# Row numbers stored later, a shorter entry to the expert search, and the first tokens turned in halves

## The chip, the cores and the metric

The kernel runs on one core of a Trainium2 chip. The metric is the time of one execution on the device, in microseconds (us). The engines are TensorE (PE in the profile, with its weight loads as PEld), VectorE (DVE), ScalarE (ACT), GpSimd (POOL) and SyncE (SP), which here only issues transfers.

## The reference

Three layers follow one another; all arrays are float32 except the dense weights, which arrive as float64.

```
attention: B=2, H=8, S=768, D=64: each query sees keys within 16 places of it and 24 block maxima
x = attention output as [N=1536, 512]
logits = x @ w_gate                       # [1536, 8]
greedy over all (token, expert) pairs in order of -logits: a token takes the expert
    if neither is used up (192 tokens per expert)
for e: y[tokens of e] = relu(x[tokens of e] @ w1[e]) @ w2[e]      # 512 -> 1024 -> 512
h = y @ w_in ; g = 0 below -1, h above 1, (h+1)^2/4 between ; out = g @ w_out   # 512 -> 2048 -> 512
```

## The kernel before

**Attention** (`attention`) works on 12 tiles of 128 tokens. Its order on every engine is the hand-written list ORDER: each entry issues a few instructions, and an engine runs its own in that order. For the last tiles the list has `x_turn` (four transposes of a finished 128x512 tile on PE), `x_store` (the tile to memory, SP), `x_out` (the transposed tile out of PSUM), `logits` (32 small products on PE) and `logits_out` (8 columns of the tile `lg`). `later 0` and `later 1` in that list build the constants of the router.

**The router** (`Router`) replaces the greedy loop by eight phases, each of which closes one expert. `scale` finds the largest absolute logit: a reduction on DVE (L482), a transpose on PE (L484), a reduction of one row (L487), a product that spreads the result over the partitions (L489), then `best` (five DVE operations, L506 to L514, that find each token's best expert) and two operations that make the factor `r` (L494, L495). `phase` then finds the closing threshold in five digits of base 32. For each digit DVE makes masks (L677), PE counts them with 12 small products (L565), DVE makes flags (L569, L572), and one more product (L575) returns the digit. After the fifth digit the phase finds the expert's members, loads the expert's number into a register, and computes the 192 row numbers `idx` (L686 on PE, L688 on ACT).

**The gather** (`Experts.fetch`): POOL issues two indirect transfers (L717, 96 rows of 2 KB each) that bring the expert's tokens from `xdram`. Beside them SP stores the row numbers to `idxd` in memory (L719, 192 pieces of 4 bytes). For the first expert SP then issues a tiny transfer out of the gathered tile (L723), which makes SP wait until the second half has landed; the rest of the expert's weights are issued behind it (L745, L747). The first half quarter of them (L744) goes out as soon as the expert is known.

**The experts** (`run_experts`): the generator `products` makes the 64 products of each expert (each shows as two instructions, a few of them L776 and L785). PE gets its order from PLAN: at every step of the router (but those named half, best, left, places) one number of PLAN is read. Until `turns`, the count of steps since the first gather was issued, passes WAIT, that many blank products (`idle`, L709: 128x512, bfloat16, result never read) fill PE; after it, that many products of the experts are issued. So PE's queue holds search and experts interleaved, and it runs in that order. The first tokens are turned by `turn(0)` at the first step past WAIT: three blanks, four transposes (L757), three blanks, four transposes, each half taken out of PSUM by ACT (L758).

**The dense layers** (`FeedForward`) take 16 steps `s`, the first half of the tokens in steps 0 to 7. Their raw weights are loaded by SP (L922, L925) and turned into float32 on DVE. `run` loads the row numbers back as `idxo` (L1208); the results are scattered to their rows by indirect transfers on POOL (L1067), the first of them after step 7.

Pools of tiles reuse memory of pools that were closed: the router's and the experts' pools lie where attention's tiles lay. The first tile of such a pool waits for everything that touched the memory under the whole pool, attention's stores of `xs` to `xdram` among it.

Of the kernel before, what the change touches and what calls it, by code (L numbers as in the profile page):

```python
# [8 lines left out]
F32 = mybir.dt.float32  # L9
# [15 lines left out]
N = B * S  # L25
DM = H * D
NT = N // 128
E = 8
# [7 lines left out]
PLAN = """  # L36
2 5 2 1 2 2 2 2 2 2 2 2 2 1 10 10 3 3 3 3 3 2 4 2 2 2 2 9 9 2 3 3 3 3 3 3 3 3 2 2 16 9 3 3 3 3 3 3 3 3 3 2 2 10
12 2 3 3 3 3 3 3 3 3 2 2 10 9 3 4 3 3 4 3 3 3 3 2 2 10 9 2 3 3 3 4 3 3 3 3 2 2 10 9 12 3
"""

WAIT = 8

# [54 lines left out]
9 1 dve; pv 11 0; x_out 8 act; pv 9 1; sums 11 0 act; norm 11 0; logits 8; sums 9 1 act; pv_out 11 0; norm 9 1;  # L97
logits_out 8 act; x_store 11; x_turn 11; pv_out 9 1; x_out 11 dve; x_turn 9; x_store 9; x_out 9 act; logits 11;
logits 9; logits_out 11 dve; logits_out 9 dve
"""  # L100


def attention(tc, ctx, C, q, k, v, wg, xdram, lg, later, order=ORDER):
# [238 lines left out]

    def x_turn(t):
        p = live["xp", t] = ptr()
        for c in range(4):
            nc.tensor.transpose(p[:, c], live["x", t][:, c * 128:(c + 1) * 128], ident)  # L346
# [4 lines left out]

    def logits(t):
        p = live["l", t] = ptr()
        for c in range(4):
            for w in range(2):
                r = slice(64 * w, 64 * w + 64)
                nc.tensor.matmul(p[r, 0, :64], live["xt", t][:, c, r], wg[:, c], start=(c == 0), stop=(c == 3))
# [4 lines left out]
    def begin():  # L362
        warm = st.tile([128, 512], BF, name="warm")
        nc.vector.memset(warm, 0.0)
        for _ in range(9):
            nc.tensor.matmul(ptr().rearrange("p a b -> p (a b)"), warm[:, :128], warm, start=True, stop=True)

        rel = st.tile([128, 96], F32, name="rel")
        for h in range(2):
            nc.gpsimd.iota(rel[64 * h:64 * h + 64], pattern=[[1, 96]], base=-16, channel_multiplier=-1,  # L370
                           allow_small_or_imprecise_dtypes=True)
        for b in range(B):
            nc.gpsimd.memset(VW[b * G][:32, 0, :, :D], 0.0)
            nc.gpsimd.memset(VW[b * G + G - 1][64:96, 3, :, :D], 0.0)
            nc.gpsimd.memset(KW[b][:, 0, :, 0, :16], 0.0)
            nc.gpsimd.memset(KW[b][:, G - 1, :, 3, 80:96], 0.0)
        nc.vector.tensor_copy(identb, ident)
        nc.vector.memset(eps, 1e-9)

        nc.vector.memset(blocks, 0.0)  # L380
        nc.vector.tensor_reduce(blocks[:, 22:24], ident[:96, 16:80].rearrange("p (b k) -> p b k", k=32), axis=AX.X, op=OP.add)
        nc.vector.tensor_reduce(strips, ident.rearrange("p (k r) -> p r k", k=4)[:, :NB], axis=AX.X, op=OP.add)
        nc.vector.tensor_tensor(rel, rel, rel, op=OP.mult)
        for j in range(3):
            nc.vector.tensor_scalar(bias[j][:, :96], rel, 256.0, NEG, op0=OP.is_ge, op1=OP.mult)
            nc.vector.memset(bias[j][:, 96:], 0.0)

        nc.vector.memset(bias[0][:64, :16], NEG)
        nc.vector.memset(bias[2][64:, 80:96], NEG)
# [17 lines left out]
class Router:  # L407
# [15 lines left out]
    def open(self, ctx):  # L423
        self.wk = ctx.enter_context(self.tc.tile_pool(name="rt_work", bufs=2, side="right"))
        self.pp = ctx.enter_context(self.tc.tile_pool(name="rt_psum", bufs=2, space=PSUM, side="right"))

    def consts(self):
# [26 lines left out]
        self.ones = st.tile([1, 128], F32, name="ones")  # L454
        g.memset(self.ones, 1.0)
        self.left = st.tile([128, E], F32, name="left")
# [18 lines left out]
    def ps(self):  # L475
        return self.pp.tile([128, 512], F32, name="rt")

    def scale(self):

        nc, wk, lg = self.nc, self.wk, self.lg  # L480
        m = wk.tile([128, 1], F32, name="m")
        nc.vector.tensor_reduce(m, lg, axis=AX.XY, op=OP.max, apply_absolute_value=True)  # L482
        p = self.ps()
        nc.tensor.transpose(p[:1, :128], m, self.C["ident"])  # L484
        yield "scale"
        m2 = wk.tile([1, 1], F32, name="m2")
        nc.vector.tensor_reduce(m2, p[:1, :128], axis=AX.X, op=OP.max)  # L487
        p = self.ps()
        nc.tensor.matmul(p[:, :1], self.ones[:1], m2, start=True, stop=True)  # L489
        yield "scale"  # L490
        v = yield from self.best(lg)
        half = KARY / 2
        r = wk.tile([128, 2], F32, name="r")
        nc.vector.tensor_scalar(r[:, 0:1], p[:, :1], 1.0 / (half - 0.25), 1e-36, op0=OP.mult, op1=OP.max)  # L494
        nc.vector.reciprocal(r[:, 1:2], r[:, 0:1])  # L495

        self.v0 = wk.tile([128, NT], F32, name="v0")
        nc.vector.tensor_scalar(self.v0, v, r[:, 1:2], half, op0=OP.mult, op1=OP.add)
        self.r = r

# [17 lines left out]
    def phase(self, k):  # L518
# [13 lines left out]
        if not last:  # L532
            oh = self.oh
            for j in range(LEVELS):
# [25 lines left out]
                if k == 0 and j == 0:  # L560
                    nc.vector.tensor_scalar(Z, self.lg, self.r[:, 1:2], KARY / 2, op0=OP.mult, op1=OP.add)
                yield "mask" if j else "first"
# [128 lines left out]
class Experts:  # L691


    def __init__(self, tc, ctx, C, xdram, w1, w2, router, ff, idxd, spare, xp):
        self.tc, self.nc, self.C, self.spare = tc, tc.nc, C, spare
        self.x, self.w1, self.w2, self.rt = xdram, w1, w2, router
        self.ff, self.idxd, self.xp = ff, idxd, xp
        self.quarters = 0
        self.post = []
        self.wk = ctx.enter_context(tc.tile_pool(name="ex_work", bufs=2))  # L700
        self.pp = ctx.enter_context(tc.tile_pool(name="ex_psum", bufs=2, space=PSUM))
        self.W, self.XG, self.XT, self.number = {}, {}, {}, {}
# [8 lines left out]
    def fetch(self, k):  # L711
# [4 lines left out]
        for h in range(2):  # L716
            nc.gpsimd.indirect_dma_start(out=self.XG[k][:, h], out_offset=None, in_=self.x,  # L717
                                         in_offset=bass.IndirectOffsetOnAxis(ap=idx[:, h:h + 1], axis=0))
        nc.sync.dma_start(bass.AP(tensor=self.idxd.tensor, offset=self.idxd.offset + k // 4 * (N // 2) + k % 4 * 96,  # L719
                                  ap=[[1, 96], [HALF, 2]]), idx)  # L720
        if k == 0:
# [75 lines left out]
def run_experts(router, ex, ff, leave, plan=PLAN):  # L797
# [37 lines left out]

    def turn(k):
        for h in range(2):
            if k == 0:
                ex.idle(3)
            ex.transposed(k, h)  # L840
        turned[0] = k + 1

# [23 lines left out]
    for r in route():  # L866
# [7 lines left out]
        if turns > WAIT:  # L874
            for _ in range(n):
                next(run, None)
        else:
            ex.idle(n)
    for n, _ in enumerate(run):
        if n % TAIL == 0 and not ff.busy:  # L880
            next(conversions, None)
# [3 lines left out]
class FeedForward:  # L885
# [6 lines left out]

    def __init__(self, tc, ctx, C, w_in, w_out, idxd, out):
        self.tc, self.nc, self.ctx = tc, tc.nc, ctx
        self.w_in, self.w_out, self.idxd, self.out = w_in, w_out, idxd, out
        self.st = ctx.enter_context(tc.tile_pool(name="ff_static", bufs=1))
# [201 lines left out]
    def early(self, spare):  # L1098

        nc, tc = self.nc, self.tc  # L1100
        self.wk = self.ctx.enter_context(tc.tile_pool(name="ff_work", bufs=2, side="right"))
        self.pp = self.ctx.enter_context(tc.tile_pool(name="ff_psum", bufs=2, space=PSUM, side="right"))
        self.half = self.st.tile([128, 1], F32, name="half")
# [20 lines left out]
    def steps(self):  # L1124
# [6 lines left out]
        for s in range(2 * P):  # L1131
            outer = self.outer(s - 1, order) if s else iter(())
            ph, sided, summed = {}, 0, 0
            for n, j in enumerate((0, 1, 4, 6, 2, 3, 5) if s == 0 else range(7)):
                if s == 0 and j in (4, 6):
# [59 lines left out]
        for t in (3, 4, 5, 0, 1, 2):  # L1195
            h = t // 3
            for _ in self.outer(2 * P - 1, ((0, h, (t,)), (1, h, (t,)))):
                pass

    def run(self, ctx):  # L1200
        nc, tc = self.nc, self.tc
        self.ww = ctx.enter_context(tc.tile_pool(name="ff_split", bufs=3))
        self.op = ctx.enter_context(tc.tile_pool(name="ff_out", bufs=1, space=PSUM))
        for i in range(2):
            for _ in self.split(0, i):
                pass
        idx = self.idx = self.st.tile([128, NT], I32, name="idxo")
        nc.sync.dma_start(idx, bass.AP(tensor=self.idxd.tensor, offset=self.idxd.offset, ap=[[1, 128], [128, NT]]))  # L1208
        for _ in self.work:
# [3 lines left out]
def build(tc, q, k, v, w_gate, w1, w2, w_in, w_out, out):  # L1213
    nc = tc.nc
    with ExitStack() as ctx:
# [17 lines left out]
        with ExitStack() as c1:  # L1233
            attention(tc, c1, C, q, k, v, wg, xdram, lg, (rt.consts, rt.consts2))
        ff = FeedForward(tc, ctx, C, w_in, w_out, idxd, out)
        c4 = ExitStack()
        xp = c4.enter_context(tc.tile_pool(name="ex_x", bufs=2, side="right"))
        rt.open(c4)
        with ExitStack() as c2:
            ex = Experts(tc, c2, C, xdram, w1, w2, rt, ff, idxd, spare, xp)  # L1240
            run_experts(rt, ex, ff, c4.close)
# [28 lines left out]
```

## Time and profile before

| what | us |
|---|---|
| median of three runs (593.78, 597.09, 1673.16) | 597.09 |
| the profiled execution | 594.48 |
| its span | 592.4 |
| PE busy in the span | 569.9 (96%) |
| DVE busy | 405.1 (68%) |
| ACT busy | 276.4 (47%) |
| POOL busy | 174.3 (29%) |

The profiled execution took 2.08 us more than its span. Times in rows count from the start of the span. A share of busy time is an average over the layers; the timeline shows which engine waits for which at one place. PE's busy time contains the blank products.

### The profile page before, as it was taken

The page shows a single profiled execution, that of the slowest core. Times are in us where ns is not written, and L with a number is a line of the kernel's source. Part 1 is how long each engine was busy: PE and PEld are TensorE (multiplying, and loading weights), DVE is VectorE, ACT ScalarE, POOL GpSimd, SP SyncE. Part 2 cuts the span into 40 slices and gives each one's busy share as a digit, 9 for nine tenths or more (in the row PEclk, how much of TensorE's full clock was granted, in tenths as well). Part 3 has the DMA queues.
Part 4 walks back from the last instruction along what each step waited for, and adds up shares of the span by engine and source line. Part 5 has one row for each costly group of instructions (what it writes and reads, how often), then busy time and mean ns, then how long its engine had stood idle before and what let it go on. Part 6 is the DMA issues. An engine that isn't in the chain of part 4 may idle for free.

```text
span 592.4 us, 11433 instructions
## 1 busy us (share of the span) xinstructions
PE 569.9 (96%) x4298; PEld 485.2 (82%) x4298; DVE 405.1 (68%) x1092; ACT 276.4 (47%) x637; POOL 174.3 (29%) x271
## 2 busy tenths in 40 slices
PE   6799998999999999999999999999999999999996
PEld 4568683478988888899999988888888888989884
DVE  6887775753665755645666898886799886666651
ACT  5576670021222222223221756566677766666653
POOL 5412100100101101113000443333355875555424
PEclk9999998999999999999999999999999999999999
DMA  9999124388738659598888232100000100000002
GB/s 214 189 207 203 38 75 143 52 284 286 231 114 280 208 108 282 108 189 221 286 284 279 88 102 89 37 2 1 1 0 1 71 37 2 0 1 1 2 0 107
DMA packets 84073, 71.42 MB, mean 121 GB/s; under 512 B 42546, under 2 KB 71218, under 8 KB 84018
## 3 DMA queue, kind: packets, MB, share of 16 engines
q1 hardware_dynamic: 81506, 64.38, 39.8%
q0 software_dynamic: 1984, 6.29, 4.2%
q8 instruction: 34, 0.56, 0.4%
q14 instruction: 21, 0.17, 0.1%
q10 hardware_dynamic: 528, 0.02, 0.1%
HBM read 64.38 MB, written 6.30 MB: 119 GB/s over the span
## 4 chain that ended last, share of the span: by engine, by line
PE 82%; DVE 10%; issue 2%; ACT 2%; POOL 1%; DMA 1%; POOLq 0%; DVEq 0%; SPq 0%
PE po L1049 18%; PE ph L1016 17%; PE acc L776 15%; PE acc L785 14%; PE rt L565 2%; PE po L318 2%; PE pt L304 2%; PE px L709 2%; PE ps L280 1%; PE ptr L212 1%; DVE gl L1032 1%; DMA nat<-in_q_dram 1%; PE px L757 1%; PE ptr L346 1%; POOL out_dram L1067 1%
## 5 line engine op out<-in xcount | busy, mean ns | idle before, releaser
L776 PE MATMUL acc<-xt,slot 128*128 128x192 f32 x512 | 94.3, 333 | 0.6 <-ACT xt L758 0.6
L785 PE MATMUL acc<-ht,slot 128*128 128x192 f32 x512 | 94.2, 332 | 0.0
L776 PEld LDWEIGHTS acc<-xt,slot 128*128 128x128 f32 x512 | 82.3, 190 | 1.3 <-ACT xt L758 0.8
L785 PEld LDWEIGHTS acc<-ht,slot 128*128 128x128 f32 x512 | 82.5, 190 | 0.5
L994 POOL TENSOR_TENSOR al<-sums,ah 128x256 fp32r<-128x256 f32 x64 | 52.8, 827 | 89.4 <-ACT ah L993 79.9
L1016 PE MATMUL ph<-yh,ah 128*128 128x384 f32 x218 | 75.1, 344 | 1.7 <-DVE c L1119 1.1
L1049 PE MATMUL po<-wl,gh 128*128 128x512 f32 x192 | 76.0, 396 | 0.3 <-POOL wl L1007 0.3
L1049 PE MATMUL po<-wh,gl 128*128 128x512 f32 x192 | 75.9, 395 | 0.0
L1049 PE MATMUL po<-wh,gh 128*128 128x512 f32 x192 | 75.8, 395 | 0.0
L1016 PE MATMUL ph<-yl,ah 128*128 128x384 f32 x218 | 73.7, 338 | 0.0
L1016 PE MATMUL ph<-yh,al 128*128 128x384 f32 x218 | 73.6, 338 | 0.0
L717 POOL DMA_INDIRECT xg<-xdram,idx x16 | 15.0, 937 | 179.9 <-ACT idx L688 59.5
L994 POOL TENSOR_TENSOR al<-slot,ah 128x256 fp32r<-128x256 f32 x48 | 41.6, 867 | 79.0 <-PE ph L1016 43.0
L1029 ACT ACTIVATE gh<-u 128x384 fp32r<-128x384 f32 x64 | 33.4, 522 | 59.0 <-DVE u L1027 58.6
L1032 DVE TENSOR_TENSOR gl<-u,gh 128x384 fp32r<-128x384 f32 x64 | 51.3, 801 | 6.8 <-ACT gh L1029 6.7
L780 ACT ACTIVATE ht<-acc 128x192 f32<-128x192 f32 x64 | 21.0, 330 | 64.0 <-PE acc L776 64.0
L1016 PEld LDWEIGHTS ph<-yh,ah 128*128 128x128 f32 x218 | 40.9, 188 | 9.9 <-DVE u L1146 3.0
L1016 PEld LDWEIGHTS ph<-yl,ah 128*128 128x128 f32 x218 | 40.9, 188 | 3.9
L1049 PEld LDWEIGHTS po<-wl,gh 128*128 128x128 f32 x192 | 36.1, 188 | 6.1 <-POOL wl L1007 0.7
L1049 PEld LDWEIGHTS po<-wh,gl 128*128 128x128 f32 x192 | 36.1, 188 | 6.0
L1016 PEld LDWEIGHTS ph<-yh,al 128*128 128x128 f32 x218 | 40.9, 188 | 0.0
L790 ACT ACTIVATE yr<-acc 128x192 f32<-128x192 f32 x32 | 10.5, 330 | 64.5 <-PE acc L785 64.5
(228 smaller groups left out, 996.0 us busy)
## 6 DMA issues: line engine op xcount, KB each, us to landing
slot<-in_moe_w_dram SPq DMA_DIRECT2D x31, 1024.0 KB, 8.3
raw<-in_moe_w_in_dram SPq DMA_DIRECT2D x16, 512.0 KB, 5.4
raw<-in_moe_w_out_dram SPq DMA_DIRECT2D x16, 512.0 KB, 5.4
vw<-in_v_dram SPq DMA_DIRECT2D x20, 192.0 KB, 5.7
nat<-in_k_dram SPq DMA_DIRECT2D x12, 256.0 KB, 5.0
nat<-in_q_dram SPq DMA_DIRECT2D x12, 256.0 KB, 5.3
xdram<-xs SPq DMA_DIRECT2D x12, 256.0 KB, 2.9
slot<-in_moe_w_dram SPq DMA_DIRECT2D x2, 512.0 KB, 5.6
```

Of the source, the lines that this page charges most:

```text
L304: nc.tensor.transpose(pt[:, c], pr[:, c], ident)
L318: nc.tensor.matmul(po[64 * w:64 * w + 64, c], pt[:, c, 64 * w:64 * w + 64], VW[b * G + i // 2][:, n, 2 * c + a], start=True, stop=True)
L565: nc.tensor.matmul(p[:KARY, :E], mk[:, t], oh[:, t], start=(t == 0), stop=(t == NT - 1))
L717: nc.gpsimd.indirect_dma_start(out=self.XG[k][:, h], out_offset=None, in_=self.x, in_offset=bass.IndirectOffsetOnAxis(ap=idx[:, h:h + 1], ...
L776: nc.tensor.matmul(p, w[:, c, f % 4 * 128:f % 4 * 128 + 128], xt[:, c], start=(c == 0), stop=(c == 3))
L780: nc.scalar.activation(ht[:, f], p, AF.Relu)
L785: nc.tensor.matmul(p, w[:, f, c % 2 * 128:c % 2 * 128 + 128], ht[:, f], start=(f == 0), stop=(f == 7))
L994: nc.gpsimd.tensor_tensor(l, x, h.bitcast(F32), op=OP.subtract)
L1016: nc.tensor.matmul(p, w[:, 128 * c:128 * c + 128], y[:, b, c], start=first and n == 0, stop=n == 5, skip_group_check=True)
L1029: nc.scalar.activation(gh, u, AF.Copy)
L1032: nc.vector.tensor_tensor(gl, u, gh.bitcast(F32), op=OP.subtract)
L1049: nc.tensor.matmul(self.po[t], x[:, c], w, start=(self.left[t] == 6 * self.PAIRS - 1), stop=(self.left[t] == 0))
```

## The change

- ORDER: a new entry `later 2` computes `first` (the five operations of `best`) for token tiles 0 to 7 on DVE, between `x_out 11` and `logits_out 11`; `x_turn 11`, `x_turn 9` and `logits 9` get one, two and one blank products ahead of them.
- `scale`: `first` is done for the last four tiles only, two operations while PE transposes and three while it spreads the maximum. The factor is folded into the spreading product: `ones` holds 1/15.75, a further product adds a tiny constant, and DVE is left with one reciprocal. `scale` has one step more, so PLAN has one number more; its first numbers are 3 2 3 where 2 5 stood.
- All pools that reuse memory are opened with `reuse_waits="tile"`: a tile waits for the tiles that lay under it alone.
- The store of the row numbers and their load back move from `fetch` and `run` to `rows`, issued by SP at dense step 5.
- WAIT is 7 instead of 8; the two halves of the first tokens are turned at steps 5 and 6 after the blanks of that step, without the six blanks of `turn(0)`. PLAN's numbers for steps 5, 6 and 8 are 2, 2 and 3, where 3, 3 and 4 stood; step 8 now issues products of the first expert.

```diff
-2 5 2 1 2 2 2 2 2 2 2 2 2 1 10 10 3 3 3 3 3 2 4 2 2 2 2 9 9 2 3 3 3 3 3 3 3 3 2 2 16 9 3 3 3 3 3 3 3 3 3 2 2 10
+3 2 3 2 1 2 2 2 2 2 2 2 2 2 1 10 10 3 3 3 2 2 2 3 2 2 2 2 9 9 2 3 3 3 3 3 3 3 3 2 2 16 9 3 3 3 3 3 3 3 3 3 2 2 10
-WAIT = 8
+WAIT = 7
+HALVES = 5, 6
...
-logits_out 8 act; x_store 11; x_turn 11; pv_out 9 1; x_out 11 dve; x_turn 9; x_store 9; x_out 9 act; logits 11;
-logits 9; logits_out 11 dve; logits_out 9 dve
+logits_out 8 act; x_store 11; x_turn 11 1; pv_out 9 1; x_out 11 dve; later 2; x_turn 9 2; x_store 9; x_out 9 act; logits 11;
+logits 9 1; logits_out 11 dve; logits_out 9 dve
...
+    def unread(p, n):
+        for _ in range(n):
+            nc.tensor.matmul(p.rearrange("p a b -> p (a b)"), live["warm"][:, :128], live["warm"], start=True, stop=True)
+
-    def x_turn(t):
+    def x_turn(t, blanks=0):
         p = live["xp", t] = ptr()
+        unread(p, blanks)
...
-    def logits(t):
+    def logits(t, blanks=0):
         p = live["l", t] = ptr()
+        unread(p, blanks)
...
-        self.wk = ctx.enter_context(self.tc.tile_pool(name="rt_work", bufs=2, side="right"))
-        self.pp = ctx.enter_context(self.tc.tile_pool(name="rt_psum", bufs=2, space=PSUM, side="right"))
+        self.wk = ctx.enter_context(self.tc.tile_pool(name="rt_work", bufs=2, side="right", reuse_waits="tile"))
+        self.pp = ctx.enter_context(self.tc.tile_pool(name="rt_psum", bufs=2, space=PSUM, side="right", reuse_waits="tile"))
...
-        g.memset(self.ones, 1.0)
+        g.memset(self.ones, 1.0 / (KARY / 2 - 0.25))
+        self.tiny = st.tile([1, 1], F32, name="tiny")
+        g.memset(self.tiny, 2.0e-35)
...
         return self.pp.tile([128, 512], F32, name="rt")
 
+    def ahead(self):
+
+        st, full = self.st, [128, NT, E]
+        self.best0 = [st.tile(s, d, name=n) for n, s, d in (("v0b", [128, NT], F32), ("w0", full, BF),
+                                                            ("mx0", [128, NT], F32), ("oh0", full, BF))]
+        for o in self.first(slice(0, 8)):
+            o()
+
+    def first(self, s):
+
+        nc, lg = self.nc, self.lg
+        v, w, mx, oh = (a[:, s] for a in self.best0)
+        full = [128, s.stop - s.start, E]
+        z, rev = lg[:, s], self.rev[:, None, :].to_broadcast(full)
+        yield lambda: nc.vector.tensor_reduce(v, z, axis=AX.X, op=OP.max)
+        yield lambda: nc.vector.tensor_tensor(w, z, v[:, :, None].to_broadcast(full), op=OP.is_equal)
+        yield lambda: nc.vector.tensor_tensor(w, w, rev, op=OP.mult)
+        yield lambda: nc.vector.tensor_reduce(mx, w, axis=AX.X, op=OP.max)
+        yield lambda: nc.vector.tensor_tensor(oh, w, mx[:, :, None].to_broadcast(full), op=OP.is_equal)
+
     def scale(self):
 
         nc, wk, lg = self.nc, self.wk, self.lg
+        rest = list(self.first(slice(8, NT)))
         m = wk.tile([128, 1], F32, name="m")
         nc.vector.tensor_reduce(m, lg, axis=AX.XY, op=OP.max, apply_absolute_value=True)
+        yield "scale"
         p = self.ps()
         nc.tensor.transpose(p[:1, :128], m, self.C["ident"])
+        for o in rest[:2]:
+            o()
         yield "scale"
         m2 = wk.tile([1, 1], F32, name="m2")
         nc.vector.tensor_reduce(m2, p[:1, :128], axis=AX.X, op=OP.max)
         p = self.ps()
-        nc.tensor.matmul(p[:, :1], self.ones[:1], m2, start=True, stop=True)
+        nc.tensor.matmul(p[:, :1], self.ones, self.tiny, start=True, stop=False)
+        nc.tensor.matmul(p[:, :1], self.ones, m2, start=False, stop=True)
         yield "scale"
-        v = yield from self.best(lg)
+        for o in rest[2:]:
+            o()
         half = KARY / 2
-        r = wk.tile([128, 2], F32, name="r")
-        nc.vector.tensor_scalar(r[:, 0:1], p[:, :1], 1.0 / (half - 0.25), 1e-36, op0=OP.mult, op1=OP.max)
-        nc.vector.reciprocal(r[:, 1:2], r[:, 0:1])
+        r = wk.tile([128, 1], F32, name="r")
+        nc.vector.reciprocal(r, p[:, :1])
 
         self.v0 = wk.tile([128, NT], F32, name="v0")
-        nc.vector.tensor_scalar(self.v0, v, r[:, 1:2], half, op0=OP.mult, op1=OP.add)
-        self.r = r
+        nc.vector.tensor_scalar(self.v0, self.best0[0], r, half, op0=OP.mult, op1=OP.add)
+        self.r, self.oh = r, self.best0[3]
 
...
         for h in range(2):
             nc.gpsimd.indirect_dma_start(out=self.XG[k][:, h], out_offset=None, in_=self.x,
                                          in_offset=bass.IndirectOffsetOnAxis(ap=idx[:, h:h + 1], axis=0))
-        nc.sync.dma_start(bass.AP(tensor=self.idxd.tensor, offset=self.idxd.offset + k // 4 * (N // 2) + k % 4 * 96,
-                                  ap=[[1, 96], [HALF, 2]]), idx)
...
-    def turn(k):
-        for h in range(2):
-            if k == 0:
-                ex.idle(3)
+    def turn(k, halves=(0, 1)):
+        for h in halves:
             ex.transposed(k, h)
-        turned[0] = k + 1
+        turned[0] = k + (halves[-1] == 1)
...
         else:
             ex.idle(n)
+            if turns in HALVES:
+                turn(0, (HALVES.index(turns),))
...
+            if s == P - 3:
+                self.rows()
...
+    def rows(self):
+
+        nc, d = self.nc, self.idxd
+        for k in range(E):
+            nc.sync.dma_start(bass.AP(tensor=d.tensor, offset=d.offset + k // 4 * (N // 2) + k % 4 * 96,
+                                      ap=[[1, 96], [HALF, 2]]), self.places[k])
+        self.idx = self.st.tile([128, NT], I32, name="idxo")
+        nc.sync.dma_start(self.idx, bass.AP(tensor=d.tensor, offset=d.offset, ap=[[1, 128], [128, NT]]))
+
     def run(self, ctx):
         nc, tc = self.nc, self.tc
-        self.ww = ctx.enter_context(tc.tile_pool(name="ff_split", bufs=3))
-        self.op = ctx.enter_context(tc.tile_pool(name="ff_out", bufs=1, space=PSUM))
+        self.ww = ctx.enter_context(tc.tile_pool(name="ff_split", bufs=3, reuse_waits="tile"))
+        self.op = ctx.enter_context(tc.tile_pool(name="ff_out", bufs=1, space=PSUM, reuse_waits="tile"))
         for i in range(2):
             for _ in self.split(0, i):
                 pass
-        idx = self.idx = self.st.tile([128, NT], I32, name="idxo")
-        nc.sync.dma_start(idx, bass.AP(tensor=self.idxd.tensor, offset=self.idxd.offset, ap=[[1, 128], [128, NT]]))
...
-            attention(tc, c1, C, q, k, v, wg, xdram, lg, (rt.consts, rt.consts2))
+            attention(tc, c1, C, q, k, v, wg, xdram, lg, (rt.consts, rt.consts2, rt.ahead))
...
```

## Rows read from the trace of the kernel before

**Rows 1.** Windows: length; PE, PEld, DVE, ACT, POOL busy; granted clock; DMA share; GB/s
```profile
99.00:102.40 3.40, 3.40 (x20) 0.86 (x19) 1.90 (x11) 0.00 (x0) 0.00 (x0) 0.51 0.00 0
124.00:586.00 462.00, 458.23 (x2789) 413.27 (x2789) 316.20 (x809) 216.56 (x499) 146.10 (x169) 1.00 0.38 115
```

**Rows 2.** Timeline, search front: start, us, engine, line, op, tiles, [idle before <-releaser]
```profile
91.20 0.17 DVE L130 COPY lg<-ptr 128x8 f32<-128x8 f32 x1 [0.84 <-PE ptr L357]
92.02 0.17 DVE L130 COPY lg<-ptr 128x8 f32<-128x8 f32 x1 [0.65 <-PE ptr L357]
92.63 0.25 DVE L482 TENSOR_REDUCE m<-lg 128x1 f32<-128x96 f32 x1 [0.45 <-DMA xdram<-xs]
92.99 0.27 PE L484 MATMUL rt<-ident,m 128*1 128x128 f32 x1 [1.01 <-DVE m L482]
93.30 0.28 DVE L487 TENSOR_REDUCE m<-rt 1x1 f32<-1x128 f32 x1 [0.41 <-PE rt L484]
93.63 0.38 PE L489 MATMUL rt<-m,ones 1*128 1x1 f32 x2
94.66 0.26 DVE L514 TENSOR_TENSOR oh<-w,mx 128x96 bf16<-128x96 bf16 x1
95.02 0.16 DVE L495 RECIPROCAL r<-r 128x1 f32<-128x1 f32 x1
96.11 0.46 PE L565 MATMUL rt<-oh,mk 128*32 128x8 bf16 x12 [0.49 <-DVE mk L677]
```

**Rows 3.** Timeline, the counts of the next three digits on TensorE
```profile
97.95 0.46 PE L565 MATMUL rt<-oh,mk 128*32 128x8 bf16 x12
99.94 0.48 PE L565 MATMUL rt<-oh,mk 128*32 128x8 bf16 x12
102.40 0.46 PE L565 MATMUL rt<-oh,mk 128*32 128x8 bf16 x12
```

**Rows 4.** Timeline: row numbers ready, their store, first gather, SP after its wait
```profile
110.80 0.17 ACT L688 ACTIVATE idx<-rt 96x2 int32<-96x2 f32 x1 [3.66 <-PE rt L686]
110.99 0.33 SPq L719 DMA_DIRECT2D idxd<-idx  x1
111.84 1.15 POOL L717 DMA_INDIRECT xg<-xdram,idx  x1 [42.63 <-DVE v L506]
120.62 0.30 SPq L723 DMA_DIRECT2D spare<-xg  x1
```

**Rows 5.** DMA issues of three windows and the page: KB each, us to landing
```profile
idxd<-idx SPq DMA_DIRECT2D x1, 0.8 KB, 6.8
xg<-xdram,idx POOLq DMA_INDIRECT x1, 8.0
xg<-xdram,idx POOLq DMA_INDIRECT x1, 5.7
xg<-xdram,idx POOLq DMA_INDIRECT x2, 12.8
xdram<-xs SPq DMA_DIRECT2D x12, 256.0 KB, 2.9
```

**Rows 6.** Windows, one microsecond in which the first gather is under way
```profile
114.00:115.00 1.00, 1.00 (x6) 0.40 (x5) 0.54 (x6) 0.00 (x0) 0.20 (x1) 1.00 0.98 33
```

**Rows 7.** Timeline of PE: blanks, a count, first half's turn, first product
```profile
116.67 0.82 PE L709 MATMUL px<-blank 128*128 128x512 bf16 x3
119.40 0.46 PE L565 MATMUL rt<-oh,mk 128*32 128x8 bf16 x12
121.52 0.50 PE L757 MATMUL px<-ident,xg 96*128 96x96 f32 x4
123.72 0.92 PE L776 MATMUL acc<-xt,slot 128*128 128x192 f32 x4 [0.58 <-ACT xt L758]
```

**Rows 8.** Timeline, dense layers: last weight loads on SP, first store on POOL
```profile
367.21 10.75 SPq L925 DMA_DIRECT2D raw<-in_moe_w_out_dram  x2
464.57 1.01 POOL L1067 DMA_INDIRECT out_dram<-slot,idxo  x1 [0.46 <-ACT slot L1064]
```

More of the change, by code (lines that the diff above doesn't have):

```diff
@@ L362, in begin @@
     def begin():
-        warm = st.tile([128, 512], BF, name="warm")
+        warm = live["warm"] = st.tile([128, 512], BF, name="warm")
         nc.vector.memset(warm, 0.0)
@@ L560, in phase @@
                 if k == 0 and j == 0:
-                    nc.vector.tensor_scalar(Z, self.lg, self.r[:, 1:2], KARY / 2, op0=OP.mult, op1=OP.add)
+                    nc.vector.tensor_scalar(Z, self.lg, self.r, KARY / 2, op0=OP.mult, op1=OP.add)
                 yield "mask" if j else "first"
@@ L691, with __init__ @@
 class Experts:
-    def __init__(self, tc, ctx, C, xdram, w1, w2, router, ff, idxd, spare, xp):
+    def __init__(self, tc, ctx, C, xdram, w1, w2, router, ff, spare, xp):
         self.tc, self.nc, self.C, self.spare = tc, tc.nc, C, spare
         self.x, self.w1, self.w2, self.rt = xdram, w1, w2, router
-        self.ff, self.idxd, self.xp = ff, idxd, xp
+        self.ff, self.xp = ff, xp
         self.quarters = 0
         self.post = []
-        self.wk = ctx.enter_context(tc.tile_pool(name="ex_work", bufs=2))
-        self.pp = ctx.enter_context(tc.tile_pool(name="ex_psum", bufs=2, space=PSUM))
+        self.wk = ctx.enter_context(tc.tile_pool(name="ex_work", bufs=2, reuse_waits="tile"))
+        self.pp = ctx.enter_context(tc.tile_pool(name="ex_psum", bufs=2, space=PSUM, reuse_waits="tile"))
         self.W, self.XG, self.XT, self.number = {}, {}, {}, {}
@@ L891, with __init__ @@
     ORDER = (0, 4, 1, 5, 3, 2, 6)
-    def __init__(self, tc, ctx, C, w_in, w_out, idxd, out):
+    def __init__(self, tc, ctx, C, w_in, w_out, idxd, out, places):
         self.tc, self.nc, self.ctx = tc, tc.nc, ctx
-        self.w_in, self.w_out, self.idxd, self.out = w_in, w_out, idxd, out
+        self.w_in, self.w_out, self.idxd, self.out, self.places = w_in, w_out, idxd, out, places
         self.st = ctx.enter_context(tc.tile_pool(name="ff_static", bufs=1))
@@ L1100, in early @@
         nc, tc = self.nc, self.tc
-        self.wk = self.ctx.enter_context(tc.tile_pool(name="ff_work", bufs=2, side="right"))
-        self.pp = self.ctx.enter_context(tc.tile_pool(name="ff_psum", bufs=2, space=PSUM, side="right"))
+        self.wk = self.ctx.enter_context(tc.tile_pool(name="ff_work", bufs=2, side="right", reuse_waits="tile"))
+        self.pp = self.ctx.enter_context(tc.tile_pool(name="ff_psum", bufs=2, space=PSUM, side="right", reuse_waits="tile"))
         self.half = self.st.tile([128, 1], F32, name="half")
@@ L1233, in build @@
         with ExitStack() as c1:
-            attention(tc, c1, C, q, k, v, wg, xdram, lg, (rt.consts, rt.consts2))
-        ff = FeedForward(tc, ctx, C, w_in, w_out, idxd, out)
+            attention(tc, c1, C, q, k, v, wg, xdram, lg, (rt.consts, rt.consts2, rt.ahead))
+        ff = FeedForward(tc, ctx, C, w_in, w_out, idxd, out, rt.idx)
         c4 = ExitStack()
-        xp = c4.enter_context(tc.tile_pool(name="ex_x", bufs=2, side="right"))
+        xp = c4.enter_context(tc.tile_pool(name="ex_x", bufs=2, side="right", reuse_waits="tile"))
         rt.open(c4)
         with ExitStack() as c2:
-            ex = Experts(tc, c2, C, xdram, w1, w2, rt, ff, idxd, spare, xp)
+            ex = Experts(tc, c2, C, xdram, w1, w2, rt, ff, spare, xp)
             run_experts(rt, ex, ff, c4.close)
```

## The prediction

> **What bounds the kernel now.** I read the windows view first. From 124 us to 586 us PE is busy for 458.23 of 462 us at the full clock [rows 1]: the expert products, the dense layers and the search's small products stand in one queue that hardly ever waits. All waits of that stretch together are 3.8 us, so an edit inside it can win little. What decides is when that queue begins with useful work: its first product starts at 123.72 [rows 7]. PE is busy before it too, but with blank products, which are filling; there the timeline shows a chain. The last logits are copied out at 92.02, the maximum is taken from 92.63, five digits follow, the first row numbers are ready at 110.97, the gather starts at 111.84, and the second half has landed when SP gets past its wait at 120.62 [rows 2 to 4].
>
> So I cost the change by how much earlier the first product starts, and carry that to the end. Sums are against the profiled execution's own 594.48 us; the median shown is 2.61 us more, the lowest run 0.70 us less.
>
> **The front of the search.** Three things happen.
>
> The wait: DVE ends its last copy at 92.19 and stands 0.45 us for an attention store before L482 [rows 2]. The store reads `xs`, and the maximum's tile is a new one of the router's pool, so this is a wait for reused memory, which "tile" takes away if no `xs` lay under it. L482 then starts right behind the copy, at 92.22 as I take it. That alone is -0.41.
>
> The transpose: before, it starts 0.36 after L482. Now three blanks of 0.22 (0.82 for three in [rows 7], the last drawn out) are ahead of it. PE has ended the logits by about 92.0, so they end at about 92.65, and the transpose starts at 92.7 instead of 92.99.
>
> The rest: the row maximum follows 0.31 behind, at 93.0. Before, five operations for all tiles stood between it and the factor and ended at 94.92, though the spread had ended at 94.01; the reciprocal came at 95.02 [rows 2]. Now eight of the twelve tiles are done before: DVE stood idle for 0.84 until 91.20, and five operations of up to 0.26 fill that and delay the copy at 91.20 by some 0.4, which nothing late waits for (the copy at 92.02 keeps its time). Of the last four tiles, three short operations run under the spread. That has one product more (0.2, half of the 0.38 for the pair of passes at L489) behind two blanks, so it ends at about 94.0, and the single reciprocal follows there. From it on all is as before: **-1.0**. Bounds: -0.4 (the wait alone) to -1.4 (the blanks cost nothing). The blanks in the logits wait with the transposes for DVE anyway; if they were late, 0.2 each.
>
> **The clock.** In 99.0 to 102.4 the granted clock is 0.51, the 1.2 GHz level [rows 1], though PE had waited at most 1.0 us at one place (ahead of the transpose) and was filled thinly before. The counts are 1.84 apart, then 1.99 and 2.46 [rows 2, 3]: 0.8 lost. The new blanks stand in just the idle places around 89 to 93, so I take it that the fall does not come: **-0.8**, bounds -0.8 and 0. The Trainium skill ("TensorE: Matmul & The Clock Gate", Loop structure matters more than you think) speaks against this: it says that copies by DVE between dense products leave PE warm and a long wait for a transfer makes it cold. By that page no blank here could matter, and the sum would be 0.8 less. The trace disagrees in so far as the clock fell with no transfer waited for in the search.
>
> **The gather.** Row numbers are then ready 1.8 earlier, and the gather starts at 110.04. It landed after 8.0 before, while the store of 0.8 KB beside it took 6.8 [rows 5], and at 114 to 115 the transfer engines were 0.98 busy moving 33 GB/s [rows 6]: busy with something that moves no bytes. The second gather, whose row numbers were stored later, needed 5.7 for its first half in spite of weights in flight [rows 5]. A plain store of 256 KB lands in 2.9; behind POOL's 1.15 that would be 4.1. So without the small writes between 4.1 and 5.7; I take 4.6, nearer to the first, as the engines are free: the first half lands at 114.6, the second, issued behind POOL's 1.15 and so some 1.3 later, at 116.0. The Trainium skill ("DMA: Bandwidth & Descriptors", Issuing engines are not separate DMA queues) holds that all issuers share the engines and that issuing elsewhere saves only the sequencer's time; by that the moved store is worth no more than its 0.33 us of issue, and the gather would land as late as before, which is the second rival.
>
> **PE's order up to the first product.** Step 5's blanks were at 116.67; they come at 114.87, and being two they end at 115.3: the first half is there, PE does not wait. Four transposes (0.50) push the next count by 0.2. Step 6: two blanks, four transposes of the half that landed at 116.0, wanted at about 116.5. The next two products are 0.45 behind in all. Step 8's place was behind the count at 119.40, so at 119.79; now it is 119.79 - 1.8 + 0.45 = 118.45, and there the first product stands instead of 123.72: 5.27 earlier. Gone from between are four blanks at step 8, six in the turn, and PE's wait for ACT (0.58); one digit's return (0.17 and its start, 0.27) now follows it instead of leading. **5.0 in all**, of which 3.2 is from this and the gather. The weights behind the gather are issued from about 116.0, 4.6 earlier than at 120.62, so they keep most of their lead over the products.
>
> **The dense layers.** Nine transfers go onto SP's queue. SP's last weight load is issued by 377.96, before dense step 5, and the first scatter is at 464.57 [rows 8]: even eight stores one after another at 6.8 are 54 us, and they overlap. Nothing is queued behind them; cost 0, bounds 0 and, if they all waited in line and the scatter with them, still 0. For the other pools' waits I take 0; below they could win at most the 3.8 us that PE waits at all, of which most is for DVE and ACT.
>
> The sum: 594.48 - 1.0 - 0.8 - 3.2 = **589.5**.
>
> **Rivals.**
> - The clock falls all the same, in this or another stretch of the thinly filled search: 590.3. For it: the fills of the digits are the same; against: the idle ahead of them is filled. This is also what the page on the clock gate gives.
> - The small writes were not what delayed the gather: it lands after 8.0, the first half at 118.04, the second 1.8 before 120.62, at 118.8. PE stands in step 5 for 2.7, and with it the search: first product at 121.2, gain 2.25: 592.2; a low clock after such a wait would take up to 1.7 more. For it: the gather reads with many packets. Against: [rows 5, 6].
> - The gain is used up later, where a transfer or DVE sets the pace and PE waits: 594.5. Against: 458.23 of 462 [rows 1], and loads that are issued as PE frees the slots.
> - The other side: the second half's transposes stand in PE's queue ahead of the second search, so a late gather holds up both. The first product then comes 2.0 behind the landing (116.5 to 118.45 above); the point from which it is slower is a landing after 10.1 us (111.34 + 10.1 + 2.0 + 0.27 is 123.72). The last gather took 12.8 [rows 5], in the middle of weight loads: first product at 126.1, 2.7 lost: 597.2. Against: here SP issues the weights only behind the gather.
>
> **The numbers.** Chances: forecast 0.48, the clock 0.25, the small writes 0.15, used up 0.09, slower 0.03. The range: from 587.0 (the bound of the front, 0.4, a faster gather than I use, some of the pool waits, and the lowest run's 0.7) to 594.0 (the third case just left out, with the second and a run above the profiled one inside). Two per cent, 11.9 us, is about what a measurement of this kernel tells from no change; no case reaches it on either side, so 0.04, 0.93 and 0.03.
>
> **What would show it.** Right: L482 about 0.2 behind the last copy with no store before it; the count of the first digit at about 95.1; counts 1.8 apart and a clock of 1.0 throughout 95 to 105; the first gather's landing under 5.7; the first L776 near 118.5, and a busy share of PE behind it as before. Wrong: a transfer named ahead of L757 on PE; a first product beyond 121; new waits behind 124; stores at step 5 that the first scatter waits for.

## The result and the profile after

| what (us) | before | after |
|---|---|---|
| median of five runs each, one chip | 594.71 | 589.16 |
| lowest | 593.69 | 587.98 |
| the profiled execution | 594.48 | 589.34 |
| its span | 592.4 | 587.6 |

The ratio is 0.9903, with a 95% interval of 0.9876 to 0.9930: some 5.8 us or 1% faster. The forecast was 589.5. One run of before, at 1673.16, is a disturbance that the ratio leaves out.

The front of the search after (timeline; columns as in [rows 2]):

```profile
91.95 0.17 DVE L131 COPY lg<-ptr 128x8 f32<-128x8 f32 x1 [0.63 <-PE ptr L364]
92.23 0.25 DVE L512 TENSOR_REDUCE m<-lg 128x1 f32<-128x96 f32 x1
92.84 0.28 DVE L520 TENSOR_REDUCE m<-rt 1x1 f32<-1x128 f32 x1
93.81 0.17 DVE L529 RECIPROCAL r<-rt 128x1 f32<-128x1 f32 x1 [0.15 <-PE rt L523]
...
92.54 0.27 PE L515 MATMUL rt<-ident,m 128*1 128x128 f32 x1
94.90 0.46 PE L599 MATMUL rt<-oh,mk 128*32 128x8 bf16 x12
```

The maximum stands 0.11 behind the end of the last copy, with no store named; in [rows 2] it was 0.44. From that copy to the first count of a digit 4.09 became 2.95.

The counts, the row numbers and the gather after (timeline of several engines):

```profile
100.26 0.46 PE L599 MATMUL rt<-oh,mk 128*32 128x8 bf16 x12
102.03 0.46 PE L599 MATMUL rt<-oh,mk 128*32 128x8 bf16 x12
...
108.67 0.17 ACT L722 ACTIVATE idx<-rt 96x2 int32<-96x2 f32 x1 [3.72 <-PE rt L720]
109.71 1.14 POOL L751 DMA_INDIRECT xg<-xdram,idx  x1 [40.81 <-DMA slot<-in_moe_w_dram]
...
114.19 0.31 SPq L755 DMA_DIRECT2D spare<-xg  x1
```

The DMA issues of the windows that hold the first gather's two halves, one answer each:

```profile
xg<-xdram,idx POOLq DMA_INDIRECT x1, 3.2
```

```profile
xg<-xdram,idx POOLq DMA_INDIRECT x1, 3.0
```

They landed after 3.2 and 3.0, where the first took 8.0 before [rows 5]. PE behind it:

```profile
114.98 0.50 PE L789 MATMUL px<-ident,xg 96*128 96x96 f32 x4
116.24 0.49 PE L789 MATMUL px<-ident,xg 96*128 96x96 f32 x4
117.89 1.24 PE L808 MATMUL acc<-xt,slot 128*128 128x192 f32 x6
```

No wait is named; the first product stands 5.83 ahead of the 123.72 of [rows 7]. Of that 0.31 is not the change's: attention's first logits came 0.31 earlier in this execution. Windows of this execution (columns as in [rows 1]):

```profile
99.00:102.40 3.40, 3.15 (x34) 1.25 (x33) 1.96 (x12) 0.00 (x0) 0.00 (x0) 1.00 0.02 5
119.00:581.00 462.00, 458.00 (x2784) 412.16 (x2784) 319.74 (x811) 216.49 (x499) 147.91 (x169) 1.00 0.35 114
311.00:335.00 24.00, 22.82 (x135) 22.12 (x133) 19.40 (x35) 11.41 (x29) 6.86 (x9) 1.00 0.55 182
```

The clock is 1.00 where it was 0.51, and 458.00 of 462 us is close to the 458.23 of [rows 1]: behind its first product PE is as full as before. Only 311 to 335 is thinner, by 0.8 than the 24 us that answer to it before:

```profile
317.00:341.00 24.00, 23.64 (x138) 22.86 (x137) 17.82 (x33) 12.01 (x30) 7.60 (x9) 1.00 0.53 172
```

### The profile page after: what moved, and what is told of

The parts are those of the page before. It is cut to its first block, busy times and chain, and to the rows that moved or that the text cites. A ratio compares the mean times of both kernels' runs of the same rounds, so it can differ in the third digit from the quotient of the medians.

```text
span 587.6 us, 11410 instructions
## 1 busy us (share of the span) xinstructions
PE 566.7 (96%) x4293; PEld 484.2 (82%) x4293; DVE 408.4 (70%) x1096; ACT 276.4 (47%) x637; POOL 176.1 (30%) x272
## 4 chain that ended last, share of the span: by engine, by line
PE 79%; DVE 11%; DMA 2%; issue 2%; ACT 2%; POOL 1%; POOLq 0%; DVEq 0%; ACTq 0%
PE po L1081 18%; PE ph L1048 17%; PE acc L808 13%; PE acc L817 13%; DMA raw<-in_moe_w_in_dram 2%; PE rt L599 2%; PE po L319 2%; PE pt L305 2%; PE ps L281 2%; PE px L743 1%; DVE slot L972 1%; PE ptr L352 1%; DVE gl L1064 1%; DVE slot L970 1%; PE ptr L174 1%
```

## The experiments

Each was profiled once and timed in three rounds (e12 in five) beside the kernel before, whose median was 594.37, 594.57 and 594.04 in the three groups (e1 to e4, e5 to e8, e10 to e13). Attention takes unequal times from one profiled execution to the next: the first product of the logits, ahead of all edits, stood between 47.46 (e1) and 49.40 (e10), at 48.08 in before and 47.77 in the changed kernel. So places are compared net of it where the text says so, and a single profile does not settle a few tenths.

**e1: the stores beside the gathers again.**

```diff
+        nc.sync.dma_start(... self.ff.idxd ..., idx)     # in fetch, beside the gather
-        for k in range(E): nc.sync.dma_start(... self.places[k])   # in rows
```

> The changed kernel with one part undone: the row numbers are stored beside the gathers again; the load back stays at dense step 5. Theory (the 192 small writes slow the gather, and PE's order hands the delay on): the first half of the first gather lands after about 8 us instead of 3.2, at some 117.7; PE waits ahead of its transposes at step 5; the first product comes at about 120.6 instead of 117.9, and the time is some 2.7 us above the changed kernel's (ratio to before about 0.995). Rival (the gather became faster for another reason, as the waits of the pools): landing 3 to 4 us, first product at 117.9, ratio 0.990.

594.69, ratio 0.9992 [0.9972, 1.0012]: the whole gain is gone, twice the 2.7 that I expected. Timeline of PE, then windows:

```profile
117.45 0.52 PE L791 MATMUL px<-ident,xg 96*128 96x96 f32 x4 [2.61 <-DMA xg<-xdram,idx]
121.08 1.33 PE L810 MATMUL acc<-xt,slot 128*128 128x192 f32 x3
```

```profile
115.00:118.60 3.60, 1.15 (x18) 0.89 (x19) 0.34 (x4) 0.49 (x1) 0.00 (x0) 1.00 0.19 49
118.60:128.90 10.30, 10.30 (x56) 7.57 (x55) 3.04 (x18) 1.15 (x3) 0.00 (x0) 0.50 0.95 322
128.90:140.00 11.10, 11.10 (x97) 10.26 (x96) 8.22 (x44) 2.42 (x8) 1.84 (x2) 1.00 0.81 268
```

The first half landed after 7.9, PE stood for 2.61, and the first product was 2.64 ahead of before's. Then the granted clock lay at 0.50, the 1.2 GHz level, for 10.3 us in which PE was busy all the time; the products that were 2.64 ahead were 0.78 behind by before's 152.9. Of these 3.42 us the changed kernel loses 0.30 at the same products at full clock, through its order (5.83 ahead becomes 5.54). So about 3.1 went on the clock, more than on the wait.

Not every execution had that stretch. The mean granted clock of each run was taken, and 10.3 us at half clock take 0.009 off it (10.3 times 0.5, over 593). Three of the ten runs had 0.998, 0.994 and 0.995, which leaves no room for it; they took 591.31, 592.50 and 594.36. The seven others, at 0.986 to 0.991, have a median of 595.06.

**e2: before, with the stores and the load back moved to dense step 5, and nothing else.**

> The kernel before with one part alone: stores and load back of the row numbers moved to dense step 5, nothing else. Theory (a faster gather is worth only what PE's order lets it start earlier): the first gather lands after about 3.2 us instead of 8.0, but the first product stays at 123.7 within 0.3 and the time is that of before, ratio 0.998 to 1.002. Rival (the stores cost time by themselves, all through the experts, on SP's queue or in memory): some us less, ratio 0.990 to 0.995.

594.66, ratio 1.0008 [0.9997, 1.0019]. The gather landed after 3.3 and 3.1, and nothing came of it: PE's order kept the half's turn where it was, and the first product with it, 0.42 behind the 123.72 of before, of which 0.37 is attention's:

```profile
124.14 0.92 PE L774 MATMUL acc<-xt,slot 128*128 128x192 f32 x4 [0.58 <-ACT xt L756]
```

The products were 0.41 late up to the last expert and 0.1 to 0.2 late in the dense layers, before and behind the step with the stores, so the moved stores cost nothing either.

**e3: the front alone** (the changed kernel with the old WAIT, PLAN, turn and place of the stores).

```diff
-3 2 3 2 1 ... 10 10 3 3 3 2 2 2 3 2 ...
+3 2 3 2 1 ... 10 10 3 3 3 3 3 2 4 2 ...
-WAIT = 7
+WAIT = 8
```

> The changed kernel with the entry to the search alone: stores beside the gathers, WAIT 8, the blanks of the turn and PLAN's numbers from the second search on as before; the new blanks, the split best and the tile waits stay. Theory: row numbers ready at about 108.8 instead of 110.97, clock 1.0 through the search, first product at about 121.6, ratio to before about 0.9965 (2.1 us). Rival (the shorter entry is taken up by the wait for the gather or by weights that come later): row numbers at 108.8 but the first product behind 123, ratio 0.999 or more.

591.94, ratio 0.9975 [0.9942, 1.0008]. The interval reaches past 1 because of one run at 596.78; the other five took 591.58 to 592.93. The first product was 2.34 ahead (1.80 net of attention), and 2.66 at the experts' end:

```profile
121.38 0.92 PE L810 MATMUL acc<-xt,slot 128*128 128x192 f32 x4 [0.58 <-ACT xt L792]
```

The clock stayed at 1.00 in the search, the gather took 7.7, and PE did not wait for it, since the turn came a step later than in e1.

**e4: the changed kernel without its new blanks.**

```diff
-x_turn 11 1; ... x_turn 9 2; ... logits 9 1;      PLAN: 3 2 3 2 1
+x_turn 11;   ... x_turn 9;   ... logits 9;        PLAN: 0 2 3 2 1
```

> The changed kernel without its new blanks: none ahead of the turns and logits of the last tiles, none ahead of the transpose of the maximum. Theory (the clock falls when the idle places from 88 to 93 are not filled): the granted clock is about 0.5 for some 3 us in the first search, row numbers 0.5 to 0.9 later than at 108.84, ratio some 0.001 above 0.990. Rival (copies by DVE leave the clock up, so that the blanks do nothing but take time): clock 1.0 throughout, row numbers at 108.7 or a little earlier, ratio 0.990.

587.76, ratio 0.9894 [0.9877, 0.9910]. The clock did not fall:

```profile
99.00:102.40 3.40, 3.15 (x34) 1.33 (x34) 1.94 (x12) 0.00 (x0) 0.00 (x0) 1.00 0.02 5
```

In this execution of the changed kernel the clock stayed up without the blanks. By the two traces they cost about 0.2 (the one ahead of the last logits); the times do not tell e4 from the changed kernel.

**e5: the pools wait as a whole again** (`reuse_waits="tile"` taken out of the nine calls).

> The changed kernel with its pools waiting as a whole again, as before, instead of tile by tile; all else as changed. Theory (the maximum's tile is a new one of a pool that lies over the attention's memory): the maximum at L512 waits again for the last attention store, some 0.4 us, row numbers 0.4 later, and that 0.4 stays to the end, since PE is busy from its first product on: 589.6. Rival 1: the dense layers' waits were shortened by it too, up to 1.5 us more there: 591. Rival 2: the maximum no longer waits in any case (its operand was free already): 589.2 and a trace like that of the changed kernel.

588.80, ratio 0.9903 [0.9877, 0.9929]. The maximum began 0.20 behind the copy's end (0.11 after) and named no store, so in this execution the store had ended or all but ended; e13 below, with the same waits, shows it again, 0.42 for `xdram`. The products stood as in the changed kernel to 0.02 us up to the last expert, though attention was 0.25 earlier here: net of it the old waits cost 0.27 in this trace, which the time does not show. The later pools' waits show no worth. In the last expert the products kept the lead that the changed kernel lost there: PE was busy for 23.68 of 24 us:

```profile
311.00:335.00 24.00, 23.68 (x140) 23.12 (x139) 19.34 (x35) 11.95 (x30) 8.38 (x9) 1.00 0.57 187
```

**e6: 96 pieces of 8 bytes beside each gather**, to neighbouring places of a scratch.

```diff
+        nc.sync.dma_start(self.pairs[96 * k:96 * k + 96], idx)
```

> The changed kernel with one more transfer beside each gather, on the same queue and at the same place as the old store of row numbers: the same 768 bytes, but to neighbouring places of a scratch, so that 96 pieces of 8 bytes are written instead of 192 of 4 bytes. (The scattered stores in the dense layers stay.) Theory that the count of small writes made the first gather late: half the pieces, half the delay, so the first half lands after 5.3 us (midway between the 3.2 of the changed kernel and the 7.4 with the store beside); PE then waits some 0.7 us ahead of the first half's transposes: 590 to 592, more if the clock falls behind the wait. Rival, that it is any store beside it, whatever its pieces: landing above 6.5, PE waits 2 us or more, 594. Rival, that it is the scattered places and not the count: landing 3.5 or less, 589.2.

589.24, ratio 0.9904 [0.9879, 0.9929]. The window with the first half's issue:

```profile
xg<-xdram,idx POOLq DMA_INDIRECT x1, 5.4
```

5.4, as the count of pieces had it. Over the first half's 3.2 without a store, that is 0.023 us for each of 96 pieces, and e1's 7.9 is 0.024 for each of 192, with the same bytes in all. The places differ as well, so the two rivals are out (places alone, any store alike), but a share of the places in the delay is not. PE's first transposes came 0.26 later than in the changed kernel, and no low clock followed.

**e7 and e8: halves and first products one and two steps of the search earlier.**

```diff
-WAIT = 7             PLAN: ... 10 10 3 3 3 2 2 2 3 2
-HALVES = 5, 6
+WAIT = 6   (e8: 5)   PLAN: ... 10 10 3 3 2 2 2 3 3 2   (e8: 3 2 2 2 3 3 3 2)
+HALVES = 4, 5   (e8: 3, 4)
```

> The changed kernel with the two halves of the first tokens turned, and the first expert's products begun, one step of the search earlier (WAIT 6, halves at steps 4 and 5). The first half's transposes then come about 1.1 us earlier on PE, near 113.9, and the first half has landed at about 112.9. Theory (PE is full from its first product on, so that product's place sets the end): no wait for the gather, first product at about 116.8, 1.1 us less: 588.1. Rival, that the loads of the dense layers' weights at 305 to 320 set the pace there, so that what comes earlier to that place waits there: the first product 1.1 earlier and the time 588.8 to 589.2. Other side: the first product waits for the first expert's weights, or PE waits for the gather and the clock falls behind that: 590 or more.

> The same by two steps of the search (WAIT 5, halves at steps 3 and 4). The first half's transposes come near 112.8, the first half has landed at about 112.9, the second at about 114.2 where it is wanted at about 114. Theory: waits of 0.3 us at most, first product at about 115.8: 587.2. Rival, the clock falls to 0.5 behind even a short wait for the gather, as it did for 10 us with the store beside the gather: 4 us lost, 591. Rival, the loads at 305 to 320 set the pace: first product 2 us earlier, 588.5 to 589.2.

e7: 587.77, ratio 0.9888 [0.9860, 0.9915]; e8: 587.78, 0.9881 [0.9855, 0.9906]. The turns and first products:

```profile
113.83 0.50 PE L789 MATMUL px<-ident,xg 96*128 96x96 f32 x4
115.03 0.55 PE L789 MATMUL px<-ident,xg 96*128 96x96 f32 x4
116.54 1.24 PE L808 MATMUL acc<-xt,slot 128*128 128x192 f32 x6
```

```profile
112.82 0.52 PE L789 MATMUL px<-ident,xg 96*128 96x96 f32 x4
114.11 0.50 PE L789 MATMUL px<-ident,xg 96*128 96x96 f32 x4
115.76 1.24 PE L808 MATMUL acc<-xt,slot 128*128 128x192 f32 x6
```

Net of 0.29 from attention, e7 began 1.07 earlier and kept 0.76 through the experts. e8 began 1.85 earlier and kept 0.43: the searches now stand behind more products, and the second gave its row numbers 0.7 later than in the changed kernel, the last 1.2 later. PE waited 0.4 once more (a product of L609 for ACT); the rest of that loss no wait in the trace names, and it stays open. The times do not tell the two from each other.

**e10 and e11: what made the clock fall in before.** e10 is before with the new blanks alone (three of them ahead of the transposed maximum); e11 is before with its pools waiting tile by tile alone.

```diff
e10: -x_turn 11; ... x_turn 9; ... logits 9;            PLAN: 2 5 2 1
e10: +x_turn 11 1; ... x_turn 9 2; ... logits 9 1;      PLAN: 3 2 5 2 1
e11: +reuse_waits="tile" in the nine calls of the change
```

> The kernel before with the new blank products alone: ahead of the last two turns, ahead of the last logits, and three ahead of the transposed maximum (these end before the maximum is there). All waits, the five operations in the front and the stores beside the gathers stay. Read in the granted clock of 95 to 105. Theory 1 (the prediction's: idle places ahead of the search made the clock fall): clock 1.0 throughout, counts 1.8 apart, row numbers 0.8 us earlier; that alone starts the first product 0.8 earlier at most, since the gather still lands late: 593.8. Theory 2 (the page's rule, no blank here matters; the shorter front kept the clock up where it stayed up): the clock falls to 0.5 to 0.56 for 3.4 us about 99 to 102.5 all the same, 594.5.

> The kernel before with its pools waiting tile by tile, and nothing else of the change. The maximum at L482 loses its wait for the attention store (0.2 to 0.45 us); PE's wait ahead of the transposed maximum shrinks from 1.0 to 0.6 to 0.8. Theory A (the clock falls behind that wait, and its length decides): clock 1.0 in 95 to 105, row numbers 1.2 earlier than before, about 593.5. Theory B (the length of the whole thin front decides, with its five operations and 6 us of small products): the clock falls all the same, 0.4 gained at the row numbers: 594.2. Rival: the later pools' waits are worth something too: 593 with products that gain behind 300.

**e13: the changed kernel without the blanks and with the pools' waits of before** (the edits of e4 and e5).

> The changed kernel without the new blanks and with its pools waiting as a whole, as before: the store's wait (0.2 to 0.45 us) ahead of the maximum is back, and nothing fills PE there, so PE waits 0.8 to 1.1 us ahead of the transposed maximum, as in the kernel before (1.0); the front stays short, with eight of twelve tiles done ahead. Theory A (the length of that wait decides on the clock): the clock falls to 0.5 within some us behind it, 3.4 us long, 0.8 to 1.7 lost: 589 to 590. Theory B (the whole thin front decides): clock 1.0 in 95 to 105, 588.0 to 588.3.

e10: 594.61, ratio 1.0005 [0.9992, 1.0018]. e11: 593.23, 0.9981 [0.9961, 1.0000]. e13: 589.70, 0.9924 [0.9906, 0.9942]. The transposed maximum in e11 and in e13, with PE's wait ahead of it and the store that DVE waited for in e13, and the window of the fall in e2 and in e10:

```profile
92.78 0.27 PE L484 MATMUL rt<-ident,m 128*1 128x128 f32 x1 [0.64 <-DVE m L482]
```

```profile
93.50 0.25 DVE L512 TENSOR_REDUCE m<-lg 128x1 f32<-128x96 f32 x1 [0.42 <-DMA xdram<-xs]
93.85 0.27 PE L515 MATMUL rt<-ident,m 128*1 128x128 f32 x1 [0.99 <-DVE v0b L501]
```

```profile
99.00:102.40 3.40, 3.04 (x21) 0.98 (x20) 1.69 (x10) 0.00 (x0) 0.00 (x0) 0.56 0.00 0
```

```profile
99.00:102.40 3.40, 3.15 (x35) 1.36 (x34) 2.12 (x14) 0.00 (x0) 0.00 (x0) 1.00 0.00 0
```

| kernel | PE's wait ahead of the maximum (us) | five operations of `best` | clock in 99.0 to 102.4 |
|---|---|---|---|
| before [rows 1, 2] | 1.01 | all in the front | 0.51 |
| e2 | 1.03 | all in the front | 0.56 |
| e11 | 0.64 | all in the front | 1.00 |
| e10 | 0.27, behind it blanks | all in the front | 1.00 |
| e13 | 0.99 | most ahead | 1.00 |
| e4 | 0.63 | most ahead | 1.00 |

In these six executions the fall came only where the wait of 1.0 and the long front stood together. But each line is one execution, and the fall is not in every execution of before. Its 3.4 us at half clock take 0.003 off a run's mean granted clock, so a mean of 0.998 or more leaves no room for it; 15 of the 49 runs of before beside the experiments had that, 10 of the 21 beside e10, e11 and e13. One execution of e10, e11 or e13 without the fall is therefore weak evidence on what kept it away. As far as it goes, the wait of 0.99 without a fall in e13 speaks against theory A, and the long front without one in e11 against theory B. Among the fourteen profiled executions the clock fell between 95 and 105 us only in the two kernels with the old front (before and e2), and in none of the twelve with any change to it. That speaks for the change to the front as a whole; which part of it is needed stays open.

Net of attention (1.32 late) e10's row numbers came 0.8 earlier, as theory 1 had it; its time does not show that: the ten runs have a higher median than before's. e11's first product came 1.15 earlier and stayed so through the experts, 0.9 of it from the clock:

```profile
122.58 0.92 PE L776 MATMUL acc<-xt,slot 128*128 128x192 f32 x4 [0.58 <-ACT xt L758]
```

e13 took the 589 to 590 of theory A, but without the fall that was to cause it: it is slower than e4 by 0.36 from the store's wait and 1.41 that its attention took longer.

**e12: e4 and e7 together.**

> The two variants that beat the changed kernel, in one: no new blanks in the front, and halves and first products a step of the search earlier. Theory (the two gains are apart: 0.46 us in the front, 0.8 behind the gather): first product 1.5 to 1.8 us before that of the changed kernel, time 587.0 (586.6 to 587.4). Rival: without blanks the clock falls in the search in some executions, 588 to 589. Rival: the second search or the loads at 305 to 320 use it up: 587.8, as with either alone.

587.48 (587.37 to 588.84), ratio 0.9889 [0.9874, 0.9905]: 0.8 us under the changed kernel by the ratios, which lies within their intervals, and not to be told from e4, e7 or e8. Net of attention its first product came 1.29 before that of the changed kernel, less than the 1.5 to 1.8 expected. The two gains don't add up to something this measurement can show.

## Why the prediction was right, point by point

- **What bounds the kernel** held: the first product's place carried through, in the main, to the end (e2, e3, e11). The first product moved by 5.83, the end of the span by 4.84. The profiled execution's time fell by 5.14; the other 0.3 lies outside the span.
- **The front, -1.0**: from the last copy to the first count -1.14. The store's wait gave 0.33 of the 0.41; the transpose came 0.31 behind the maximum's start, so the three blanks held up nothing; from the maximum of the row (L487, now L520) to the reciprocal 1.72 became 0.97. Count at 94.90, forecast 95.1.
- **The clock, -0.8**: from the first count to the row numbers 14.69 became 13.77, so -0.92, and 1.00 throughout. The size held against this one execution of before, but at least 15 of 49 executions of before had no such fall to win back, and e10's time shows no gain. The reason, the blanks, is not shown: in the one execution of e10 the clock stayed up with them alone, but in the changed kernel it stayed up without them (e4). The Trainium skill ("TensorE: Matmul & The Clock Gate", Loop structure matters more than you think) has PE go cold behind a long wait for a transfer. e1 agrees, with 0.50 behind 2.61 us. Before, with 0.51 where PE had waited 1.01 for DVE, goes beyond it. That no transfer was waited for in the search, as the prediction says, holds for PE alone: DVE had waited 0.45 for a store ahead of the maximum [rows 2].
- **The gather**: 3.2 where I took 4.6 within 4.1 to 5.7; the row of a plain store with POOL's issue added was too long a bound. The error cost nothing: the half was there at 112.9, wanted at 114.98. The cause, small writes under way, is shown by e1 and e2, and e6 fits their count. The Trainium skill ("DMA: Bandwidth & Descriptors", Issuing engines are not separate DMA queues) has all transfers interleave on shared engines; e6 agrees, 0.8 KB beside it costing 2.2. I had read from it that the store's place was worth its issue alone. But the store was moved in time, not to another queue, so the rule never spoke against it.
- **PE's order**: 118.45 forecast, 117.89 measured; 0.33 of that is the earlier row numbers. Through the experts 6.06 stood, where I had 5.0: PE's wait for a digit (0.7 before at L588) is gone as well.
- **The second rival** was mispriced. With the gather late, the median is not 592.2, nor at most 1.7 more, but 594.69 (e1): the low clock behind the wait took about 3.1 where the prediction had up to 1.7. Only runs without it came near the price, 591.31 and 592.50.
- **"Used up later"** took 0.83 of the 6.06 at 311 to 335, where DVE waited for raw weights and PE for DVE, and 0.4 in the dense layers, which was not traced. The 0.83 is that execution's: e5 to e8 did not lose it.

```profile
319.27 0.43 DVE L968 TENSOR_SCALAR slot<-raw 128x512 int32<-128x512 int32 x1 [1.43 <-DMA raw<-in_moe_w_in_dram]
320.56 0.44 PE L1048 MATMUL ph<-yh,ah 128*128 128x384 f32 x1 [0.87 <-DVE u L1180]
```

- **The sum** came out within 0.2 of the profiled 589.34 partly by luck: 1.06 more than forecast was won up to the experts, and 1.22 of it was lost behind 311, so the two errors cancelled.
- **The dense layers' stores, 0**: shown by e2. The eight were issued from 372.79, the load back at 386.39, the first scatter at 459.47:

```profile
372.79 6.17 SPq L1238 DMA_DIRECT2D idxd<-idx  x8
386.39 0.38 SPq L1241 DMA_DIRECT2D idxo<-idxd  x1
```

## What to carry to other kernels

When an engine is full from some point on, cost a change by how much earlier that point comes, and check by experiment that nothing behind it loses the lead. In this kernel a transfer that landed sooner was worth nothing until the order of its reader was moved up (e2), and moving the reader up without it was worth nothing either (e1, against e3): the two halves of such a change are to be judged together. Ask of every wait on TensorE not only how long it is, but at which clock the work behind it runs.

## What the runs showed that I had not expected

- 192 writes of 4 bytes beside a gather of 96 rows of 2 KB put its landing from 3.2 to 7.9 us, and 96 writes of 8 bytes to 5.4: some 0.024 us a piece in both.
- Behind a wait of 2.61 us came 10.3 us at half clock with PE busy throughout (e1, in the profiled execution and in at most seven of its ten runs), while a delay of 0.26 at the same place was followed by none (e6).
- Executions of one kernel differ in whether the clock falls: 15 of 49 runs of before had too high a mean clock for the fall of [rows 1].
- The same attention took up to 1.9 us more in one execution than in another, a third of this change's whole gain.
